# Linear attention feeding a GEGLU block: all of the first batch's q read ahead of the weights, two tiles normalised at once, and a new order of the weight loads

## The chip, the cores and the metric

The kernel runs on 1 core of one Trainium2 chip. The metric is device microseconds (us) of one execution; the profiled span is about 2 us shorter than the time of the same execution. The five engines are called as in the profile: PE (TensorE), DVE (VectorE), ACT (ScalarE), POOL (GpSimd) and SP (SyncE, here only an issuer of transfers).

## The reference

Eight batches of eight heads, 576 positions, 64 channels. A linear ("cosformer") attention is followed by a GEGLU feed-forward block over all 4608 tokens.

```python
def phi(x, c, s):                       # c, s: cosine and sine of the position
    r = np.maximum(x, 0.0)
    return np.concatenate([r * c, r * s], axis=-1)
q_p, k_p = phi(q, cos_w, sin_w), phi(k, cos_w, sin_w)
kv  = np.einsum('bhsf,bhsd->bhfd', k_p, v)
z   = np.sum(k_p, axis=2)
num = np.einsum('bhsf,bhfd->bhsd', q_p, kv)
den = np.einsum('bhsf,bhf->bhs', q_p, z)[..., None] + 1e-06
x   = (num / den).transpose(0, 2, 1, 3).reshape(B * S, H * D)   # 4608 x 512
out = (gelu(x @ w_gate) * (x @ w_val)) @ w_out                  # 512 -> 1536 -> 512
```

## The kernel before

The tokens are worked through in nine blocks of 512. A block needs the normalised attention output x of its tiles (128 tokens each), turned to channel-first (xT). Then come twelve "gate/value" units (`gv_unit`, PE, then GELU on ACT and a product on DVE) and four output parts (`o_part`, PE) with the third weight, `wo`. Block 0 is the start-up stage: attention of batch 0, the weights and the first gate/value units all compete there. Block 0's output parts are interleaved with attention of batch 1; after that each block's work is interleaved with attention of the next batch.

First, loads are issued from two places. SP loads batch 0, and POOL's queue loads the weights (turning float32 into bfloat16 on the way) and q, k and v of batches 1 and 2:

```python
load(nc.sync, "k", 0, 0, 2); load(nc.sync, "k", 0, 2, 4)
load(nc.sync, "v", 0, 0, 2)
load(nc.sync, "q", 0, 0, NP, 0, 2)                 # two of nine runs of q
# ... v, then two more runs of q
nc.gpsimd.tensor_copy(gate, phi["k", 0][:, 3, 0, 0:1])   # weights start after k is prepared
load_w(0, 2); load_w(2, 2)
load(nc.gpsimd, "q", 0, 0, NP, JA, R)              # the other five runs of q
load_w(4, 2); load_w(6, 2); load_w(8, 2); load_w(10, 2)
# ... q(1), k(1), wo rows 0-3, v(1), wo rows 4-7, q(2)
for m in (0, 2):
    cast_v(1, m, m + 2, pool_copy)                 # v(1) to bfloat16, on POOL itself
# ... wo rows 8-11, k(2), v(2)
```

A "run" of q is the part that belongs to one ninth of the 576 positions (`R` is nine, `JA` four), and q(1) stands for q of batch 1. A "row" of `wo` is 128 of its 1536 rows, so an output part of four rows is four matmuls. POOL works in program order. Its issue of a transfer waits until the eighth transfer before it has landed (the releasers in the trace show it), so POOL's waits tell when transfers landed.

Second, the preparation of q and k: per batch, nine cosine operations on DVE and nine sine operations on ACT, each 128x256, float32 in and bfloat16 out.

Third, the order of work between block 0's last gate/value unit and block 1:

```python
order = (
    [("o", 0, 0), ("k",), ("o", 1, 0), ("q", 0), ("o", 2, 0), ("q", 1), ("o", 3, 0)]
    + [("o", 0, 4), ("q", 2), ("o", 1, 4), ("kv",), ("q2", 0, 5), ("o", 2, 4)]   # o(t, 4): wo rows 4-7
    + [("nm", 0, 6), ("o", 3, 4), ("nm", 1, 2), ("o", 0, 8), ...]
    # ...
    + [("xt", 2, 4), ("xt", 3, 0), ("o", 3, 8), ("q2", 5, 9)])
# ... "k": k(1) preparations; "q": q(1) turned on PE, copied by DVE or ACT; "q2": sines of q(2) on ACT
# ... "kv": the k-v product; "nm": attention of one tile (PE), normalised on DVE; "xt": x turned on PE
prep("q", 2, 0, range(R))          # nine cosines of q(2) on DVE
cast_v(2, 0, 2, pool_copy)
cast_v(2, 2, 4, pool_copy)
```

Fourth, what block 1 starts with. SP turns q of batch 2 by two transposing transfers and then loads batch 3:

```python
if n == 1 and jt == 0:
    turn_x(1, NT - 1)
    turn_q(b)          # two dma_start_transpose on SP, from qp(2) to qT(2)
    loads(b + 1)       # q(3), k(3), v(3), on SP behind them
```

## Time and profile before

| | before |
|---|---|
| time, median of 3 runs | 333.44 us (333.24 to 333.95) |
| profiled span | 331.5 us |
| PE busy | 320.4 us (97%) |
| chain of waits that ended last | 84% PE, 6% DMA, 5% DVE |
| first gate/value matmul of block 0 | 14.60 us |
| first output matmul of block 0 | 44.30 us |

The page of before, cut to its head and its chain of waits. The columns of the engine lines are busy time, share of the span and number of instructions.

```profile
span 331.5 us, 6342 instructions
...
PE 320.4 (97%) x2441; PEld 163.2 (49%) x2441; DVE 172.3 (52%) x416; ACT 159.7 (48%) x340; POOL 27.2 (8%) x44
...
PE 84%; DMA 6%; DVE 5%; ACT 2%; POOL 1%; issue 1%; SPq 0%; DVEq 0%
```

PE bounds the kernel, so the time can fall only where PE idles or does dummy matmuls (on a tile of zeros; nobody reads the result). That is the first 44 us, and a few waits after them. The timeline of before: its columns are start (us), length (us), engine, line, operation, count, and in brackets the idle time before and what ended it.

```profile
14.60 0.60 PE L349 MATMUL ps<-xT,wg_sb 128*128 128x128 bf16 x4
...
30.93 0.75 POOL L98 DMA_DIRECT2D wo_sb<-in_moe_w_out_dram  x1 [0.62 <-DMA wv_sb<-in_moe_w_val_dram]
...
42.10 1.15 POOL L179 CAST vx<-vf 128x1152 bf16<-128x1152 f32 x1 [7.13 <-DMA vf<-in_v_dram]
42.31 1.33 DVE L162 TENSOR_SCALAR qp<-qf,cos_t 128x256 bf16<-128x256 f32 x2
43.58 1.15 POOL L179 CAST vx<-vf 128x1152 bf16<-128x1152 f32 x1 [0.34 <-DMA vf<-in_v_dram]
44.30 1.89 PE L375 MATMUL ps<-wo_sb,hT 128*128 128x512 bf16 x8
...
46.15 2.97 DVE L162 TENSOR_SCALAR kp<-kf,cos_t 128x256 bf16<-128x256 f32 x9
47.78 1.89 PE L375 MATMUL ps<-wo_sb,hT 128*128 128x512 bf16 x8
50.30 0.38 PE L204 MATMUL ps<-ident,qp 128*128 128x128 bf16 x4 [0.63 <-DVE qT L433]
51.48 1.33 PE L241 MATMUL ps<-vx,kp 64*128 64x65 bf16 x72
...
60.05 2.45 DVE L162 TENSOR_SCALAR qp<-qf,cos_t 128x256 bf16<-128x256 f32 x9
62.73 8.37 SPq L193 DMA_TRANSPOSE qT<-qp  x2
75.15 0.40 PE L282 MATMUL ps<-kv_sb,qT 128*128 128x65 bf16 x7 [1.09 <-DMA qT<-qp]
```

DVE prepares the cosines of q(2) in 2.45 us, and when the last is done SP issues the transposes of q(2) at 62.73 us. PE needs their result at 74.1 us and gets it at 75.15 us.

### The profile page before, as it was taken

Reading aid. Unit: us, or ns where it says so; the run is one execution under the profiler, and the core shown is the slowest. Engines: PE = TensorE matmul, PEld = TensorE weight load, DVE = VectorE, ACT = ScalarE, POOL = GpSimd, SP = SyncE. Lnnn points to the kernel's source line nnn. Section 1 sums busy time; section 2 is a strip of 40 time slices with the busy share of each in tenths; the row PEclk is TensorE's granted clock in tenths of the full one; section 3 lists DMA queues with packets and bytes.
Section 4 is the critical chain, followed back from the end, with each engine's and each line's share of the span. In section 5 each row is a group of like instructions: output and inputs, shape, how many; then the busy total and the mean of one; then the engine's idle time right before and its main releaser. Section 6 shows DMA issues by size and latency. Waiting matters only on the chain.

```text
span 331.5 us, 6342 instructions
## 1 busy us (share of the span) xinstructions
PE 320.4 (97%) x2441; PEld 163.2 (49%) x2441; DVE 172.3 (52%) x416; ACT 159.7 (48%) x340; POOL 27.2 (8%) x44
## 2 busy tenths in 40 slices
PE   8888999999999999999999999999999999999995
PEld 3577555445455445544554455445544444444443
DVE  5776595848846854755375537562632322223211
ACT  8654584957653752754365436553232222322220
POOL 2954161100000000000000000000000000000000
PEclk9999999999999999999999999999999999999999
DMA  7999998799599999979947995780421221111124
GB/s 268 194 235 289 277 301 309 139 147 367 113 146 368 168 134 335 254 119 239 330 80 118 228 334 81 122 128 13 81 55 38 45 47 32 34 32 32 34 64 95
DMA packets 67918, 53.24 MB, mean 161 GB/s; under 512 B 44080, under 2 KB 53040, under 8 KB 67888
## 3 DMA queue, kind: packets, MB, share of 16 engines
q1 hardware_dynamic: 57936, 40.25, 52.0%
q0 software_dynamic: 9792, 12.45, 16.5%
q8 instruction: 19, 0.31, 0.4%
q10 hardware_dynamic: 160, 0.13, 0.2%
q14 instruction: 11, 0.09, 0.1%
HBM read 37.75 MB, written 9.44 MB: 142 GB/s over the span
## 4 chain that ended last, share of the span: by engine, by line
PE 84%; DMA 6%; DVE 5%; ACT 2%; POOL 1%; issue 1%; SPq 0%; DVEq 0%
PE ps L349 51%; PE ps L375 26%; PE ps L282 3%; DMA qT<-qp 3%; PE ps L241 2%; DMA wv_sb<-in_moe_w_val_dram 2%; DMA kf<-in_k_dram 1%; DVE kp L169 1%; DVE kp L162 1%; DVE qp L162 1%; PE ps L626 1%; DVE hT L358 1%; ACT kp L160 1%; POOL wg_sb L94 1%; DVE qT L433 0%
## 5 line engine op out<-in xcount | busy, mean ns | idle before, releaser
L358 DVE TENSOR_TENSOR hT<-gel,ps 128x512 bf16<-128x512 f32 (+2 forms) x119 | 75.9, 638 | 133.5 <-PE ps L349 129.7
L357 ACT ACTIVATE gel<-ps 128x512 f32<-128x512 f32 (+2 forms) x119 | 66.4, 558 | 114.8 <-PE ps L349 114.3
L349 PE MATMUL ps<-xT,wv_sb 128*128 128x512 bf16 (+2 forms) x476 | 112.8, 359 | 1.2 <-DMA wv_sb<-in_moe_w_val_dram 0.9
L349 PE MATMUL ps<-xT,wg_sb 128*128 128x512 bf16 (+2 forms) x476 | 112.9, 359 | 1.0 <-DVE xT L334 0.7
L375 PE MATMUL ps<-wo_sb,hT 128*128 128x512 bf16 x420 | 106.0, 379 | 0.1
L349 PEld LDWEIGHTS <-wv_sb 128*128 128x128 bf16 x476 | 45.5, 98 | 49.7 <-DMA wv_sb<-in_moe_w_val_dram 1.1
L349 PEld LDWEIGHTS <-wg_sb 128*128 128x128 bf16 x476 | 44.8, 98 | 48.1 <-issue 0.9
L375 PEld LDWEIGHTS <-hT 128*128 128x128 bf16 x420 | 38.4, 98 | 41.0 <-issue 0.4
L384 ACT COPY o_sb<-ps 128x512 f32<-128x512 f32 x34 | 20.0, 587 | 31.8 <-PE ps L375 31.8
L160 ACT ACTIVATE qp<-qf,sin_t 128x256 bf16<-128x256 f32 x70 | 30.7, 502 | 0.4 <-DMA qf<-in_q_dram 0.4
L160 ACT ACTIVATE kp<-kf,sin_t 128x256 bf16<-128x256 f32 (+1 forms) x75 | 30.5, 482 | 0.7 <-DMA kf<-in_k_dram 0.7
L295 DVE TENSOR_TENSOR x_sb<-ps,rec 128x512 bf16<-128x512 f32 x39 | 27.0, 691 | 1.3
L162 DVE TENSOR_SCALAR qp<-qf,cos_t 128x256 bf16<-128x256 f32 x72 | 22.6, 366 | 0.1
L282 PEld LDWEIGHTS <-qT 128*128 128x128 bf16 x312 | 15.0, 98 | 9.1 <-DMA qT<-qp 1.4
L162 DVE TENSOR_SCALAR kp<-kf,cos_t 128x256 bf16<-128x256 f32 x63 | 18.7, 355 | 0.0
L282 PE MATMUL ps<-kv_sb,qT 128*128 128x65 bf16 x312 | 16.8, 194 | 1.2 <-DMA qT<-qp 1.1
L140 PE MATMUL ps<-dummy 128*128 128x512 bf16 x33 | 10.1, 439 | 1.5 <-POOL dummy L114 1.5
L250 ACT CAST kv_sb<-ps 128x260 bf16<-128x260 f32 x14 | 4.6, 382 | 13.0 <-PE ps L241 13.0
L241 PEld LDWEIGHTS <-kp 64*128 64x128 bf16 x504 | 8.5, 94 | 3.0 <-issue 3.0
L179 DVE CAST vx<-vf 128x1152 bf16<-128x1152 f32 (+2 forms) x13 | 9.6, 737 | 0.6 <-DMA vf<-in_v_dram 0.5
L241 PE MATMUL ps<-vx,kp 64*128 64x65 bf16 x504 | 9.3, 191 | 0.0
L294 DVE RECIPROCAL rec<-den 128x8 f32<-128x8 f32 x39 | 7.9, 203 | 1.3
(57 smaller groups left out, 92.8 us busy)
## 6 DMA issues: line engine op xcount, KB each, us to landing
out_dram<-o_sb SPq DMA_DIRECT2D x70, 128.0 KB, 2.4
kf<-in_k_dram SPq DMA_DIRECT2D x12, 576.0 KB, 6.6
vf<-in_v_dram SPq DMA_DIRECT2D x11, 576.0 KB, 9.3
qf<-in_q_dram SPq DMA_DIRECT2D x10, 576.0 KB, 5.2
qf<-in_q_dram POOLq DMA_DIRECT2D x4, 576.0 KB, 12.8
kf<-in_k_dram POOLq DMA_DIRECT2D x4, 576.0 KB, 9.8
vf<-in_v_dram POOLq DMA_DIRECT2D x4, 576.0 KB, 12.2
wg_sb<-in_moe_w_gate_dram POOLq DMA_DIRECT2D x6, 256.0 KB, 9.2
```

The lines of the kernel that those rows point to most:

```text
L140: nc.tensor.matmul(bank(to), lhsT=dummy[:, 0:128], rhs=dummy, start=True, stop=True)
L160: nc.scalar.activation(o, i, AF.Relu, scale=tab[:, j:j + 1])
L162: (eng or nc.vector).tensor_scalar(o, i, 0.0, tab[:, j:j + 1], op0=ALU.max, op1=ALU.mult)
L179: copy(vx_tiles[b % 2][:, m0:m1, j0:j1, 0:D], staged["v", b][:, m0:m1, j0 * D:j1 * D].rearrange("p m (j d) -> p m j d", d=D),)
L241: nc.tensor.matmul(bank(6 + i)[:, m * (D + 1):(m + 1) * (D + 1)], lhsT=kp[rr, m, j, :], rhs=vx[rr, m, j, :], start=(j == 0), stop=(j == R ...
L282: nc.tensor.matmul(bank(b0 + h // 4)[:, (h % 4) * (D + 1):(h % 4 + 1) * (D + 1)], lhsT=q_cols(b, t, h), rhs=kv_sb[b][:, h // 2, h % 2, :], ...
L295: nc.vector.tensor_tensor(x, nm[:, :, :, 0:D], rec[:, :, :, None].to_broadcast([128, 2, 4, D]), op=ALU.mult,)
L349: nc.tensor.matmul(bank(b0 + g)[:, 0:w], lhsT=wt[:, ct, js], rhs=xt[:, ct, c0:c0 + w], start=(ct == 0), stop=(ct == CT - 1),)
L357: nc.scalar.activation(gel[:, 0:w], bank(b0)[:, 0:w], AF.Gelu)
L358: nc.vector.tensor_mul(hT[n][:, jt, c0:c0 + w], gel[:, 0:w], bank(b0 + 1)[:, 0:w])
L375: nc.tensor.matmul(bank(to), lhsT=hT[n][:, jt, tt * 128:(tt + 1) * 128], rhs=wo_sb[:, jt, :], start=(jt == 0), stop=(jt == JT - 1),)
L384: copy(o_sb, bank(to))
```

## The change

Its intent: in block 0, read all of q before any weight, so that attention of tiles 0 to 3 can be done while the weights land; normalise tiles 0 and 1 together; gate the weights on the first cast of v instead of on k; and load `wo` ahead of batch 2. The diff, cut to its core:

```diff
     load(nc.sync, "k", 0, 0, 2)
     load(nc.sync, "k", 0, 2, 4)
+    load(nc.sync, "q", 0, 0, NP, 0, JA)
     load(nc.sync, "v", 0, 0, 2)
-    load(nc.sync, "q", 0, 0, NP, 0, 2)
-    ... (v in two pieces, q runs 2-3)
+    load(nc.sync, "v", 0, 2, 4)
+    load(nc.sync, "q", 0, 0, NP, JA, R)
...
+    def nm_pair(b, t, firsts):      # matmuls of two tiles into four banks
+        ...
+        nc.vector.tensor_scalar_add(den, nm[:, :, :, D], EPS)     # 128 x 16
+        nc.vector.reciprocal(rec, den)
+        ...                         # one product per tile
...
-    nc.gpsimd.tensor_copy(gate, phi["k", 0][:, 3, 0, 0:1])
+    nc.gpsimd.tensor_copy(gate, vx_tiles[0][:, 0, 0, 0:1])
     load_w(0, 2)
     load_w(2, 2)
-    load(nc.gpsimd, "q", 0, 0, NP, JA, R)
-    load_w(4, 2) ... load_w(10, 2)
-    # then q(1), k(1), wo 0-3, v(1), wo 4-7, q(2), [cast v(1)], wo 8-11, k(2), v(2)
+    for part in range(2):
+        prep("q", 0, part, (8,), eng=nc.gpsimd)
+    for jt in (4, 6, 8, 10):
+        load_w(jt, 2)
+    # then q(1), wo 0-3, k(1), v(1), wo 4-7, wo 8-11, q(2), k(2), v(2), [cast v(1)]
...
     # block 0: the new order of PE's work
+    nm_pair(0, 0, (6, 4))
+    ... (all eight q transposes, x transposes of tiles 0 and 1, nm of tile 2)
     gv_unit(0, 0, 0, 128)
     gv_unit(0, 1, 0, 128)
+    nm_unit(0, 3, 6)
+    gv_unit(0, 0, 128, 128)
+    gv_unit(0, 1, 128, 128)
+    gv_unit(0, 2, 0, HALF) ...      # units of 256 and 512 columns from here on
```

From block 0's first output part on, the order of PE's work is the same in both kernels.

## The prediction

> **What bounds the kernel now.** TensorE. The page gives PE 97% busy (320.4 of 331.5 us) at full granted clock; the chain of waits is 84% PE. From 44.2 us, where block 0's last gate/value matmul ends on PE's timeline, the order is the same in both kernels. Up to there the useful PE work is about 20.7 us of gate/value matmuls (12 x 1.73) plus about 6.5 us of attention and transposes. The rest is start-up: nothing useful before 9.36 us, first gate/value matmul at 14.60 us, and some 4 us of holes after that (0.93 us on a value weight at 18.2, 0.7 us on an xT copy at 27.9, about 1.5 us where 128-column units wait for PSUM banks).
>
> **What the change does.** It moves all work of tiles 0-1 (q transposes of runs 0-7, normalisation, x transposes) before the first gate/value unit. nm_pair saves one 0.17 us add and one 0.20 us reciprocal. Preparing run 8 of q moves to POOL. 33 dummies become 30 (0.22 us each when warm).
>
> Costs: the weights are gated on the first cast of v instead of k. In the trace 576 KB land on the SP queue per 1.9 us (k half 4.6, v half 8.4 us). In the new order I estimate: q part 1 at 8.2, v halves at 10.1 and 12.0, q part 2 at 14.2 to 15.2 us (it then shares the DMA engines with the weights; the Trainium skill, "DMA: Bandwidth & Descriptors", section "Queues, rings and completion order", says each DMA engine round-robins between queue rows; no run here shows the split). The weights start at about 11.0 instead of 8.2 us, but total bytes are equal, so the last weight pair lands near 30.5 us as before (30.9, from POOL's waits).
>
> The new critical path is DVE: after q part 2 it does five preparations (0.31 each), the pair's add and reciprocal (0.45), two multiplies (0.69, 0.62), a qT copy (0.4); then PE's nm of tile 2 (0.26) and a dummy. That puts the first gate/value unit at 18.5 to 19.4 us, 4 to 5 us LATER than now. After it remain 20.7 + about 2.3 us of PE work and about 0.8 us of holes (PSUM banks, while DVE does nm of tiles 2 and 3): 23.8 us. Block 0 then ends at 42.3 to 43.2 instead of 44.2 us: gain 1 to 2 us.
>
> **Afterwards.** wo rows 4-11 land before q of batch 2, which I estimate at 51.8 instead of 49.5 us, just when ACT wants it (53.4 less the shift). The waits on qT (0.6 us at 50.3 on DVE, 1.1 us at 75.1 on the DMA transpose) shift and stay. Net there 0 to -0.5 us.
>
> **Predicted: 331.9 us, 8 in 10 between 330.5 and 333.4.** Faster by over 2% 0.02, within 2% 0.965, slower 0.015.
>
> **Right or wrong by:** first gate/value matmul at 18.5-19.4 us on PE's timeline, hardly any hole over 0.5 us after 22 us; the pair normalisation starting at 15.8-16.8 us behind the q preparations; no PE wait on weights; block 0 ending at 42-43 us; the 75 us wait moved by the same shift.
>
> **What would make it wrong:** q part 2 much later than 15 us or weights late (gain lost); q part 2 at 13.5 us (gain over 2.5 us); PE's clock falling in the sparse stretch 9 to 18 us (the Trainium skill, "TensorE: Matmul & The Clock Gate", Part 1, names idle windows of about 3.4 us; the before trace shows no drop with holes under 0.9 us); q of batch 2 late enough to widen the 75 us wait.

## More of the kernel before

At 44.30 us PE starts block 0's output parts. The second half of the group at 47.78 us, from about 48.65 us, is the first use of `wo` rows 4-7. Those were issued by POOL at 30.93 us, and PE does not wait for them.

(The two casts on POOL, at 42.10 and 43.58 us, will matter later. Beside the first, two cosines of q(1) took 1.33 us, where the pair before them took 0.61; the cosines of k(1) come behind both casts.)

## The result, and the profile after

| | before | after |
|---|---|---|
| time, median | 333.38 us (4 runs, 333.24 to 333.95) | 333.65 us (4 runs, 333.51 to 334.12) |
| ratio, with its 95% interval | | 1.0007 (0.999 to 1.0025) |
| profiled span | 331.5 us | 331.6 us |
| first gate/value matmul of block 0 | 14.60 us | 17.71 us |
| first output matmul of block 0 | 44.30 us | 40.80 us |
| SP issues the transposes of q(2) | 62.73 us | 63.13 us |

A ratio here is the mean time of one kernel's fast runs over the mean of the other's in the same rounds, so it is not quite the ratio of the medians quoted. The time did not move: the predicted gain of 1.5 us is absent, although the start gained 3.5 us. The page of after:

```profile
span 331.6 us, 6186 instructions
...
PE 317.8 (96%) x2360; PEld 161.0 (49%) x2398; DVE 169.1 (51%) x400; ACT 159.8 (48%) x335; POOL 29.0 (9%) x45
...
PE 78%; DMA 13%; POOL 3%; ACT 2%; issue 1%; DVE 1%; SPq 0%; DVEq 0%
```

More of the chain of waits now runs through transfers (13%, after 6%), 5% of the span through a load of `wo`. Such a share counts a transfer from its issue on and is not PE's wait; PE's waits are read off the timeline. (Part of the fall in PE's busy time is matmul records missing from the trace; the waits below don't rest on it.) The timeline of after:

```profile
15.17 0.16 DVE L316 TENSOR_SCALAR den<-ps 128x16 f32<-128x16 f32 x1
...
17.71 0.39 PE L375 MATMUL ps<-xT,wg_sb 128*128 128x128 bf16 x4
...
32.07 0.75 POOL L98 DMA_DIRECT2D wo_sb<-in_moe_w_out_dram  x1 [0.64 <-DMA wv_sb<-in_moe_w_val_dram]
...
40.80 1.89 PE L401 MATMUL ps<-wo_sb,hT 128*128 128x512 bf16 x8
...
42.63 2.62 DVE L161 TENSOR_SCALAR kp<-kf,cos_t 128x256 bf16<-128x256 f32 x9
...
46.20 2.25 POOL L178 CAST vx<-vf 128x1152 bf16<-128x1152 f32 x2
47.62 1.86 PE L401 MATMUL ps<-wo_sb,hT 128*128 128x512 bf16 x4 [2.31 <-DMA wo_sb<-in_moe_w_out_dram]
49.71 1.59 PE L401 MATMUL ps<-wo_sb,hT 128*128 128x512 bf16 x4
51.24 1.33 PE L240 MATMUL ps<-vx,kp 64*128 64x65 bf16 x72
...
58.27 1.15 POOL L178 CAST vx<-vf 128x1152 bf16<-128x1152 f32 x1 [9.81 <-PE ps L401]
59.58 1.15 POOL L178 CAST vx<-vf 128x1152 bf16<-128x1152 f32 x1 [0.16 <-DMA vf<-in_v_dram]
59.81 3.16 DVE L161 TENSOR_SCALAR qp<-qf,cos_t 128x256 bf16<-128x256 f32 x9
63.13 8.26 SPq L192 DMA_TRANSPOSE qT<-qp  x2
75.25 0.40 PE L281 MATMUL ps<-kv_sb,qT 128*128 128x65 bf16 x7 [1.42 <-DMA qT<-qp]
```

The lead of after over before, read off the same work in the two traces, goes like this:

- First output part: 44.30 less 40.80, 3.50 us ahead.
- First use of `wo` rows 4-7: before at about 48.65 us, after at 47.62 us, 1.03 us ahead. PE stood for 2.31 us, because those rows landed at 47.6 us. They were issued 1.14 us later than before (32.07 against 30.93 us), and PE now wanted them at 45.3 us.
- The k-v product: 51.48 less 51.24, 0.24 us ahead. The output part behind the hole took 1.86 us and the next 1.59 us, where four such matmuls take 1.03 us. Before, in its turn, had a 0.63 us wait here that after does not have.
- The issue of q(2)'s transposes: 62.73 less 63.13, 0.40 us behind. DVE's nine cosines began 0.24 us earlier, but they took 3.16 instead of 2.45 us, while POOL cast v(2).
- First use of the transposed q(2): 75.15 against 75.25 us. PE now waits 1.42 instead of 1.09 us. Nothing of the lead is left.

The slow matmuls have their reason in the clock. This is the view by windows of after; the columns are window, length, busy time and instructions of PE, PE's weight loads, DVE, ACT and POOL, then granted clock, DMA share and GB/s.

```profile
46.00:47.00 1.00, 0.00 (x0) 0.00 (x0) 0.38 (x1) 0.00 (x0) 1.00 (x2) 1.00 1.25 213
47.00:48.00 1.00, 0.38 (x1) 0.10 (x1) 0.00 (x0) 0.00 (x0) 1.00 (x2) 0.72 1.21 260
48.00:49.00 1.00, 1.00 (x4) 0.43 (x3) 0.00 (x0) 0.00 (x0) 0.45 (x1) 0.50 1.16 379
49.00:50.00 1.00, 1.00 (x7) 0.58 (x6) 0.05 (x1) 0.00 (x0) 0.00 (x0) 0.50 1.00 393
50.00:51.00 1.00, 1.00 (x4) 0.29 (x2) 0.38 (x1) 0.00 (x0) 0.00 (x0) 0.57 1.05 415
```

After the hole the granted clock is half for about 3.4 us. The lost clock in these windows adds up to 0.28 + 0.50 + 0.50 + 0.43 = 1.71 us, or 0.5% of the span, and indeed three of the four runs of after have a mean granted clock of 0.994 or 0.995.

### The profile page after: what moved, and what is told of

Its sections match the earlier page's. It is cut to its first block, busy times and chain, and to the rows that moved or that the text cites. A ratio compares the mean times of both kernels' runs of the same rounds, so it can differ in the third digit from the quotient of the medians.

```text
span 331.6 us, 6186 instructions
## 1 busy us (share of the span) xinstructions
PE 317.8 (96%) x2360; PEld 161.0 (49%) x2398; DVE 169.1 (51%) x400; ACT 159.8 (48%) x335; POOL 29.0 (9%) x45
## 3 DMA queue, kind: packets, MB, share of 16 engines
q0 software_dynamic: 9648, 11.80, 15.8%
## 4 chain that ended last, share of the span: by engine, by line
PE 78%; DMA 13%; POOL 3%; ACT 2%; issue 1%; DVE 1%; SPq 0%; DVEq 0%
PE ps L375 46%; PE ps L401 26%; DMA wo_sb<-in_moe_w_out_dram 5%; DMA wv_sb<-in_moe_w_val_dram 3%; PE ps L281 3%; DMA qT<-qp 3%; PE ps L240 2%; DMA vf<-in_v_dram 2%; POOL wg_sb L94 1%; POOL wv_sb L95 1%; PE ps L624 1%; POOL qp L161 1%; ACT qp L159 1%; ACT gel L383 1%; ACT kp L159 0%
## 5 line engine op out<-in xcount | busy, mean ns | idle before, releaser
L384 DVE TENSOR_TENSOR hT<-gel,ps 128x512 bf16<-128x512 f32 (+2 forms) x114 | 75.0, 660 | 133.0 <-PE ps L375 131.7
L383 ACT ACTIVATE gel<-ps 128x512 f32<-128x512 f32 (+2 forms) x114 | 65.6, 575 | 112.0 <-PE ps L375 109.9
L375 PE MATMUL ps<-xT,wg_sb 128*128 128x512 bf16 (+2 forms) x451 | 111.5, 368 | 0.5
L375 PE MATMUL ps<-xT,wv_sb 128*128 128x512 bf16 (+2 forms) x445 | 110.5, 368 | 0.4
L401 PE MATMUL ps<-wo_sb,hT 128*128 128x512 bf16 x400 | 104.5, 383 | 3.7 <-DMA wo_sb<-in_moe_w_out_dram 2.3
L375 PEld LDWEIGHTS <-wv_sb 128*128 128x128 bf16 x456 | 44.0, 98 | 49.6 <-DMA wv_sb<-in_moe_w_val_dram 0.3
L375 PEld LDWEIGHTS <-wg_sb 128*128 128x128 bf16 x456 | 43.4, 98 | 47.4 <-issue 0.3
L410 ACT COPY o_sb<-ps 128x512 f32<-128x512 f32 x34 | 20.0, 588 | 31.6 <-PE ps L401 30.5
L159 ACT ACTIVATE kp<-kf,sin_t 128x256 bf16<-128x256 f32 (+1 forms) x75 | 30.5, 483 | 0.3 <-DMA kf<-in_k_dram 0.3
L139 PE MATMUL ps<-dummy 128*128 128x512 bf16 x28 | 9.1, 484 | 1.5 <-POOL dummy L113 1.5
L178 DVE CAST vx<-vf 128x1152 bf16<-128x1152 f32 x12 | 9.2, 770 | 0.8 <-DMA vf<-in_v_dram 0.8
L292 DVE TENSOR_SCALAR den<-ps 128x8 f32<-128x8 f32 x38 | 6.1, 160 | 5.1 <-PE ps L281 5.0
## 6 DMA issues: line engine op xcount, KB each, us to landing
vf<-in_v_dram POOLq DMA_DIRECT2D x4, 576.0 KB, 14.2
```

The costliest lines, as they stand in the source:

```text
L139: nc.tensor.matmul(bank(to), lhsT=dummy[:, 0:128], rhs=dummy, start=True, stop=True)
L159: nc.scalar.activation(o, i, AF.Relu, scale=tab[:, j:j + 1])
L178: copy(vx_tiles[b % 2][:, m0:m1, j0:j1, 0:D], staged["v", b][:, m0:m1, j0 * D:j1 * D].rearrange("p m (j d) -> p m j d", d=D),)
L375: nc.tensor.matmul(bank(b0 + g)[:, 0:w], lhsT=wt[:, ct, js], rhs=xt[:, ct, c0:c0 + w], start=(ct == 0), stop=(ct == CT - 1),)
L383: nc.scalar.activation(gel[:, 0:w], bank(b0)[:, 0:w], AF.Gelu)
L384: nc.vector.tensor_mul(hT[n][:, jt, c0:c0 + w], gel[:, 0:w], bank(b0 + 1)[:, 0:w])
```

## The experiments

**Theories.** Q: PE's lead is given back because other streams do not start earlier, namely the loads on POOL's queue and the work that hangs on them, and the end of the span is set by those. In its simplest form the one hole on `wo` rows 4-7 is the whole loss. R: the loss lies elsewhere (the half clock; the single late chain that ends in q(2)'s transposes; the new order of loads as such; POOL's extra work), and removing the `wo` wait changes nothing. In what follows T is the time at which SP issues the transposes of q(2), and "before" is the kernel before on the same chip in the same rounds. All edits are to the kernel after, unless said otherwise.

### 1. The wait for wo rows 4-7: load them earlier (wo4_early)

```diff
-    for name in ("k", "v"):
-        for m in (0, 2):
-            load(nc.gpsimd, name, 1, m, m + 2)
+    for m in (0, 2):
+        load(nc.gpsimd, "k", 1, m, m + 2)
     load_wo(4, 4)
+    for m in (0, 2):
+        load(nc.gpsimd, "v", 1, m, m + 2)
```

> The changed kernel with one edit: wo rows 4-7 are loaded ahead of v of batch 1 instead of behind it. Theory Q (the load queue: the 3.4 us won by 41 us is handed back because wo rows 4-7 land at 47.5 us, behind q, wo 0-3, k and v of batch 1): the rows land at about 43.8 us, PE's 2.3 us wait for them and the half clock at 48-51 us are gone; instead v of batch 1 lands near 47.4 us and PE waits 0.5 to 1.5 us for its cast before the kv of batch 1. Time 330.5 to 332.3. Rival R (what sets the time is the DMA transpose of q of batch 2, landing at 75.2 us whatever came before, with PE waiting for it): the wait at 75 us grows by what was won, time 333.3 to 333.8.

Measured 332.67 us (332.11 to 333.73), ratio 0.9961 (0.9929 to 0.9993). The `wo` wait is gone, but against before only 0.9 us (medians) to 1.3 us (the ratio) came of it, a little less than expected. PE now waits 0.5 us for POOL's cast of v(1), 0.6 us for an output copy that stands behind ACT's sines of q(2), and 1.3 us for an x tile at 80.15 us. T moved from 63.13 us (62.21 in the control of experiment 4) only to 61.59 us. The wait is a part of the loss; it isn't the whole.

### 2. The half clock: fill the hole with dummies (warm_hole)

```diff
         if what == "o":
             o_part(...)
+        if (what, *a) == ("o", 3, 0):
+            dummies(10, 2)
```

> The changed kernel with 10 dummy matmuls (2.2 us) put into PE's hole before wo rows 4-7, so that the clock does not fall. Theory C (the half clock at 48-51 us is a loss of its own, about 1.5 us of PE time): clock 1.00 throughout, time 332.0 to 332.6. Theory R (absorbed: one of the four runs of the changed kernel had the clock at 1.00 and was no faster, 333.7): clock 1.00, PE reaches the nm of batch 2 about 1.4 us earlier and waits that much longer there, time 333.2 to 333.8.

Measured 333.62 us (332.94 to 334.89), ratio 0.9985 (0.9948 to 1.0022). The granted clock stayed at 1.00 through the stretch, and the output part behind it took its normal time. Yet the end did not come earlier: T was 62.24 us, and PE waited 0.5 us for a qT copy and 1.6 us for an x tile later. So the half clock costs nothing of its own that five rounds can see (the interval reaches 0.5% below before); what it takes, a later wait would take. This trace also shows a second thing: one sine preparation of k(1) on DVE, normally 0.34 us, lasted 2.91 us from 45.42 us, while POOL cast v(1) from 45.93 to 48.18 us. I come back to it in experiment 8.

### 3. POOL's preparation of run 8 (run8_back) and the order of loads (old_order)

```diff
# run8_back
-    for part in range(2):
-        prep("q", 0, part, (8,), eng=nc.gpsimd)
...
     gv_unit(0, 3, 0, HALF)
+    prep("q", 0, 0, (8,))
+    prep("q", 0, 1, (8,), eng=nc.scalar)

# old_order: the kernel after with before's order of POOL's loads behind the weights
-    # q(1), wo 0-3, k(1), v(1), wo 4-7, wo 8-11, q(2), k(2), v(2), [cast v(1)]
+    # q(1), k(1), wo 0-3, v(1), wo 4-7, q(2), [cast v(1)], wo 8-11, k(2), v(2)
```

> The changed kernel with run 8 of q prepared on VectorE and ScalarE behind the first half block, as before, not on POOL ahead of the third weight pair. Theory Q: the weight issue is not held for 2.6 us at 14.0-16.6 us, the DMA stream runs about 0.7 us earlier, wo rows 4-7 land near 46.8 us, PE's wait for them shrinks from 2.3 to about 1.6 us; time 332.7 to 333.4. If POOL's detour cost the stream nothing (the four weights in flight kept it busy), the wait stays at 2.3 us and the time at 333.6.

Measured 332.90 us (332.63 to 334.36), ratio 0.9973 (0.994 to 1.0006). With POOL free, the weights and all behind them came about 1.1 us earlier, and the `wo` wait fell from 2.31 to 1.45 us. But POOL's casts came earlier too (45.10 us) and met the nine cosines of k(1), which took 5.05 us instead of 2.62; PE then waited 1.1 us for a qT copy, and the half clock came anyway.

> The changed kernel with POOL's load order of before from batch 1 on (q, k, wo 0-3, v, wo 4-7, q of batch 2, the casts of v, wo 8-11, k, v). wo 4-7 stands behind the same bytes in both orders, so Theory Q says: it lands at 47.5 us again, the same 2.3 us wait and half clock; the reordering did not make the hole. q of batch 2 lands about 2.5 us earlier and the transposes of q of batch 2 may start up to 0.4 us sooner: time 333.1 to 333.7. If the reordering itself is to blame, the wait goes away and the time is under 332.

Measured 333.52 us (332.72 to 334.18), ratio 0.9982 (0.995 to 1.0014). Going back to the old order does not bring the missing gain. My expectation of an unchanged 2.3 us wait was wrong: it was 1.28 us. Rows 4-7 landed 1.2 us earlier here, behind the same transfers as in after. Most of that may be scatter: four other runs with after's loads waited 1.51 to 1.87 us (after_again, v2_cast_dve, q2cos_late, cast1_act), so the 2.31 us of the first profile is the extreme. One difference stays untested: after's POOL had issued k(2) and half of v(2) by 43.41 us, while rows 4-7 were still on their way; in old_order they come behind the casts, from 45.82 us.

### 4. A control, and T moved alone (after_again, q2cos_late, v2_cast_dve)

after_again is the kernel after, unchanged, on the chip of the other two.

> The changed kernel itself, unedited, as the control on the same chip as the next three. Every theory: 333.4 to 334.1, a wait of 1.5 to 2.5 us for wo rows 4-7 at about 45 us, the DMA transposes of q of batch 2 issued at about 63 us.

Measured 334.24 us (332.94 to 334.72), ratio 0.9993 (0.9963 to 1.0022). The profiled execution had a different mixture of waits than the first one: 1.64 us for `wo`, 0.85 us for a qT copy, no half clock, 1.90 us for an x tile at 81.35 us, and only 0.2 us for the transposed q(2). The sum comes to much the same. A single hole is not a stable property of this kernel, so none of them is likely to be the whole cause. The x tile stands behind ACT, which waited 1.86 us for q(3), until 77.75 us. SP had issued that load at 71.28 us, behind the transposes of q(2), so this wait hangs on T as well.

```diff
# q2cos_late: the last of nine cosines of q(2), and all that hangs on it, one step later
-    prep("q", 2, 0, range(R))
+    prep("q", 2, 0, range(R - 1))
...
                 if n <= 2 and jt < 3:
                     prep_third("k", b, jt)
+                if n == 1 and jt == 0:
+                    prep("q", 2, 0, (R - 1,))
+                    turn_q(b)
+                    loads(b + 1)

# v2_cast_dve: v(2) cast on DVE in units 2 and 3 of block 1
-    cast_v(2, 0, 2, pool_copy)
-    cast_v(2, 2, 4, pool_copy)
...
+                if n == 1 and jt in (2, 3):
+                    cast_v(b, 2 * jt - 4, 2 * jt - 2, dve_copy)
```

> The changed kernel with the last (ninth) cosine preparation of q of batch 2 moved on VectorE behind the first k third of batch 2, some 1.8 us later; nothing else depends on it but the DMA transposes of q of batch 2. Theory T (in all six profiles so far the end of the kernel follows the issue of those transposes, within about 0.7 us: before 62.7 us, after 63.1, wo rows earlier 61.6): issue at 64.7 to 65.1 us, PE's wait for the transposed q grows from 1.4 to about 3 us, time 1.4 to 2.0 us above the control. Rival (PE's own work and holes up to 60 us set the time, the transposes only follow): wait grows but is regained, time within 0.5 us of the control.

Measured 335.83 us (334.88 to 336.97), ratio 1.0045 (1.0014 to 1.0076), 1.6 us above the control. T was 63.35 us, 1.1 us later than in the control, where I had expected 1.8. The first use of the transposed q(2) in the control, then T and that use in q2cos_late:

```profile
72.91 0.40 PE L281 MATMUL ps<-kv_sb,qT 128*128 128x65 bf16 x7 [0.21 <-DMA qT<-qp]
...
63.35 9.49 SPq L192 DMA_TRANSPOSE qT<-qp  x2
73.99 0.40 PE L281 MATMUL ps<-kv_sb,qT 128*128 128x65 bf16 x7 [1.70 <-DMA qT<-qp]
```

PE's own work is untouched by this edit, and each of its six runs is slower than each of the control's. So what SP issues at T does hold the end: the transposes, and the loads of batch 3 that stand behind them. The two are not separated.

> The changed kernel with the cast of v of batch 2 taken off POOL and put on VectorE in gate/value units 2 and 3 of block 1, where VectorE has room. Theory L (a POOL cast holds VectorE's preparations up: nine cosine preparations took 3.16 us beside it, 2.45 us without): they take 2.4 to 2.5 us, the transposes of q of batch 2 are issued at about 62.4 to 62.7 us instead of 63.1, time 0.3 to 0.7 us below the control. If the lock is not it: 3.1 us again, no change.

Measured 332.75 us (331.97 to 334.81), ratio 0.9966 (0.993 to 1.0002), in the medians 1.5 us below the control; I had expected 0.3 to 0.7. In the means it is 0.9 us, since two of the six runs, at 334.67 and 334.81 us, gained nothing. The nine cosines of q(2) took 2.44 us as before the change, and T was 61.40 us. POOL's cast of v(2) beside them is probably a second part of the loss; the interval just reaches 1.

### 5. The hole removed without touching a load (wo_no_wait)

This kernel is wrong (relative error 0.28): block 0 multiplies with rows 0-3 of `wo` where it should use rows 4-7. All loads are as in after.

```diff
-                rhs=wo_sb[:, jt, :],
+                rhs=wo_sb[:, jt % 4 if n == 0 and 4 <= jt < 8 else jt, :],
```

> The changed kernel, wrong on purpose: block 0 multiplies with wo rows 0-3 again where it should use rows 4-7, so it does not wait for them; every load stays where it was. Isolates the wait. Theory Q with T: the 1.6 to 2.3 us wait goes, but VectorE's k preparations (held by the POOL cast of v) then hold the copy of qT and PE waits 1.5 us or more there; the transposes of q of batch 2 are issued at 61.0 to 62.3 us instead of 62.2 to 63.1; time 0 to 1.0 us below the control (332.9 to 333.8 where before is 333.5). If the wait for wo alone ate the 3.4 us: 330.5 to 331.5.

Measured 333.96 us (333.14 to 334.87), ratio 1.0014 (0.9997 to 1.003): no gain at all. The timeline of this kernel shows where the hole went.

```profile
53.44 2.10 ACT L159 ACTIVATE qp<-qf,sin_t 128x256 bf16<-128x256 f32 x5 [3.33 <-DMA qf<-in_q_dram]
55.45 1.04 ACT L410 COPY o_sb<-ps 128x512 f32<-128x512 f32 x2
56.06 0.38 PE L356 MATMUL ps<-ident,x_sb 128*128 128x128 bf16 x4 [2.29 <-ACT o_sb L410]
...
63.23 8.28 SPq L192 DMA_TRANSPOSE qT<-qp  x2
```

ACT works in program order. It reached the sines of q(2) early, stood 3.33 us until q(2) landed at 53.4 us, did five sines, and only then copied the output parts out of the banks that PE needed. PE's hole of 2.31 us reappears as one of 2.29 us, again with a reduced clock behind it, and T is where it was. PE is faster up to a fixed arrival, whichever load arrives next. I had expected the cast of v(1) to be what holds PE here. It was not: the cast began at 46.38 us, when the preparations of k(1) were done.

### 6. The new load order alone, and the old gate (before_new_order, gate_k)

```diff
# before_new_order: the kernel before with after's order of POOL's loads and casts
# gate_k: the kernel after
-    nc.gpsimd.tensor_copy(gate, vx_tiles[0][:, 0, 0, 0:1])
+    nc.gpsimd.tensor_copy(gate, phi["k", 0][:, 3, 0, 0:1])
```

> The kernel BEFORE with only the new load order on POOL's queue (wo rows 8-11 ahead of batch 2, casts of v last). Theory: the order by itself wins nothing, since PE there comes to wo rows 4-7 at 48.6 us, after they land; v and q of batch 2 land later and the POOL casts of v of batch 2 move on to VectorE's cosines of q. Time 0 to 0.8 us above before, no wait for wo rows.

Measured 334.43 us (333.88 to 337.4), ratio 1.0037 (1.0009 to 1.0066). By itself the new order costs about 0.9 us in the medians, slightly more than expected: v(1) is now cast at 44.62 us, where one cosine of q(1), begun at 44.89 us, is held for 2.13 us, and PE waits 1.15 us for it.

> The changed kernel with the weight loads gated on the preparation of k, as before, so that they start at about 8 instead of 10.7 us. Theory Q: the DMA engines' gap at 11-13 us closes, the stream runs 0.5 to 1.2 us earlier and the wait for wo rows 4-7 shrinks to about 1 us, but q part 2 and v share the engines and land 0.5 to 1.5 us later, so block 0 ends that much later. Time within 0.7 us of the control. If the late gate was the cause of the lost gain: 331.5 or less.

Measured 332.90 us (331.37 to 334.0), ratio 0.9978 (0.9957 to 0.9999). The weights' issue moves from 10.71 to 8.09 us, the first gate/value matmul from 17.71 to 16.87 us and the first output part from 40.80 to 39.87 us, yet the median gains only some 0.6 us against before. The `wo` wait is down to 0.72 us and a DVE wait of 1.66 us stands in its place: again k(1)'s cosines beside POOL's casts, 5.07 us. (The trace is of the fastest of the six runs, 331.37 us; the next was at 332.56.)

### 7. All holders taken away (best1, best2, best3, best2_again)

best1 combines wo4_early, run8_back and v2_cast_dve with two more edits; best2 also moves ACT's sines of q(2) out of the way of the output copies; best3 is best2 with gate_k's edit.

```diff
# best1, besides wo4_early, run8_back and v2_cast_dve
-    for m in (0, 2):
-        cast_v(1, m, m + 2, pool_copy)
...     # behind the second group of q(1) transposes in the order
+            if a[0] == 1:
+                for m in (0, 2):
+                    cast_v(1, m, m + 2, act_copy)
...     # preparation of q(3) one unit later in block 1
-        t_kv, t_nm, t_q, t_k = {1: (4, 6, 7, 12), ...
+        t_kv, t_nm, t_q, t_k = {1: (4, 6, 8, 12), ...

# best2, besides best1: the sines of q(2) behind the first copies, two of them on DVE
-    ("kv",), ("q2", 0, 5), ("o", 2, 4) ... ("o", 1, 8) ... ("o", 3, 8), ("q2", 5, 9)
+    ("kv",), ("o", 2, 4) ... ("o", 1, 8), ("q2", 0, 3) ... ("o", 3, 8), ("q2", 3, 7)
     prep("q", 2, 0, range(R))
+    prep("q", 2, 1, (7, 8))
```

> A version meant to beat both: the changed kernel with wo rows 4-7 ahead of v of batch 1, run 8 of q off POOL, the cast of v of batch 1 on ScalarE and that of batch 2 on VectorE, and the preparation of q of batch 3 one unit later. Theories Q, L and T together: no wait for wo rows, none over 0.4 us for the casts, transposes of q of batch 2 issued at 60.0 to 61.0 us; time 330.3 to 331.5. If the end is set elsewhere: 332.5 or more.

Measured 331.09 us (330.59 to 331.61), ratio 0.9906 (0.9877 to 0.9936), T at 60.27 us. The wait of experiment 5 is left: PE stands 1.8 us for output copies behind ACT's sines.

> best1 with ScalarE's sines of q of batch 2 moved behind the first two output copies (best1 held PE 1.8 us there) and two of the nine sines on VectorE. Theory T: PE's 1.8 us wait is gone but only an earlier issue of the transposes counts: 59.3 to 60.3 us against 60.27, time 330.2 to 331.2. If PE's wait itself counted: 329.3 to 329.9.

Measured 329.30 us (328.71 to 330.04, 4 runs), ratio 0.9866 (0.9847 to 0.9885), outputs correct. The timeline of best2:

```profile
41.18 1.89 PE L401 MATMUL ps<-wo_sb,hT 128*128 128x512 bf16 x8
...
42.85 2.45 DVE L161 TENSOR_SCALAR kp<-kf,cos_t 128x256 bf16<-128x256 f32 x9
...
47.65 1.33 PE L240 MATMUL ps<-vx,kp 64*128 64x65 bf16 x72
...
56.23 2.44 DVE L161 TENSOR_SCALAR qp<-qf,cos_t 128x256 bf16<-128x256 f32 x9
59.72 8.29 SPq L192 DMA_TRANSPOSE qT<-qp  x2
72.02 0.40 PE L281 MATMUL ps<-kv_sb,qT 128*128 128x65 bf16 x7 [0.64 <-DMA qT<-qp]
```

Here the lead of the start is kept. Against before it is 3.12 us at the first output part (44.30 less 41.18), 3.0 us at T (62.73 less 59.72), 3.13 us at the transposed q(2), and 3.3 us at the end of the span (331.5 less 328.2).

One expectation failed here. If only T counted, the time was to be 330.2 to 331.2 us; if PE's wait of 1.8 us in best1 counted by itself, 329.3 to 329.9. T came where I had put it, yet the time came at the edge of the second range: against best1 the ratio fell by 0.0040, or 1.3 us, while T and the span of the profiled executions fell by 0.5 us. (best2's was the slowest of its four runs.) So T, read off one execution, does not tell the median to better than a microsecond.

> best2 a second time, on the same chip as best3, since its first job gave only four runs: 328.7 to 330.1 where before is near 333.5, ratio 0.985 to 0.990.

Measured 329.49 us (328.89 to 330.67), ratio 0.9874 (0.9845 to 0.9903), on another chip: best2 holds.

> best2 with the weight loads gated on k as in the kernel before (start at about 8 us, the DMA gap at 11-13 us closed). Theory Q: the stream runs about 1 us earlier, q of batch 2 lands earlier, first gate/value unit at about 16.9 us, transposes issued at 58.7 to 59.5 us, time 0.3 to 1.2 us below best2 on the same chip.

Measured 329.43 us (328.81 to 330.56), ratio 0.9863 (0.9833 to 0.9893): no clear gain over best2 in the same rounds (0.06 us in the medians, 0.4 in the ratios), where I had hoped for 0.3 to 1.2 us. Its first output part, at 41.55 us, was not earlier than that of best2 (41.18 us), so the start gain seen in gate_k does not show there. But its profiled execution is not a typical one: it was the slowest of the six, the granted clock was 0.50 from 11.2 to 14.6 us, and the first gate/value matmul came at 18.55 us (17.31 in best2). The four runs with a mean clock of 1.00 lay between 328.81 and 329.85 us, so a gain of some tenths is not excluded.

### 8. Which holders are enough (wo_last, wo_last_cast, cast1_act, both)

best2 changes six things at once. The last four kernels ask for the smallest set. wo_last is wrong (relative error 0.37): block 0 uses rows 0-3 of `wo` three times, and rows 4-11 are loaded last, so that neither the `wo` wait nor the late q(2) can hold PE. cast1_act is the kernel after with v(1) cast on ACT as in best1; wo_last_cast and both add this edit to wo_last and to wo4_early.

```diff
# wo_last
-                rhs=wo_sb[:, jt, :],
+                rhs=wo_sb[:, jt % 4 if n == 0 else jt, :],
...
-    load_wo(4, 4)
-    load_wo(8, 4)
     for name in ("q", "k", "v"):
         for m in (0, 2):
             load(nc.gpsimd, name, 2, m, m + 2)
+    load_wo(4, 4)
+    load_wo(8, 4)
```

> The changed kernel, wrong on purpose: block 0 multiplies with wo rows 0-3 three times, and rows 4-11 (2 MB read) are loaded last on POOL's queue, behind batch 2, where nothing waits for them in time. It takes from the stream what stands between v of batch 1 and q of batch 2. If the load stream as a whole is what ate the 3.4 us: no wait for wo rows, none for q of batch 2 (which lands about 47 to 49 instead of 52 to 53.4 us, so ScalarE is not held as in wo_no_wait), the DMA transposes of q of batch 2 issued at 60.0 to 61.3 us, time 330.8 to 332.0. If the time stays at 333.3 or more, the stream is not the cause.

Measured 334.19 us (330.68 to 335.0), ratio 0.9997 (0.9956 to 1.0039). My expectation failed clearly. PE has no wait on a load left between 40 and 90 us, and still nothing is gained. The view of the tile of prepared k in wo_last, with durations in ns as minimum, median and maximum, and then its timeline:

```profile
L161 DVE TENSOR_SCALAR kp<-kf,cos_t x9: 334/341/2806, 42.9 to 45.2; 128x256 bf16<-128x256 f32 x9
```

```profile
45.62 2.25 POOL L178 CAST vx<-vf 128x1152 bf16<-128x1152 f32 x2
49.20 0.38 PE L203 MATMUL ps<-ident,qp 128*128 128x128 bf16 x4 [2.66 <-DVE qT L455]
63.14 8.11 SPq L192 DMA_TRANSPOSE qT<-qp  x2
```

The median of the nine cosines is 0.34 us. The last, begun at 45.22 us, takes 2.81 us, to 48.02 us, which is 0.15 us after the end of POOL's second cast (47.87 us). PE then waits 2.66 us for the qT copy that DVE owes it, and the clock halves again. In warm_hole, run8_back, gate_k and before_new_order the held operation also ends 0.15 to 0.16 us after the end of the second cast, so the pair of casts holds it.

> wo_last (wrong on purpose, 2 MB of wo rows out of the way) with the cast of v of batch 1 on ScalarE instead of POOL. In wo_last no load held PE any more, yet five of six runs stayed at 333.7 to 335.0 and one was at 330.68: VectorE's nine k preparations took 5.13 us there beside POOL's 2.25 us of casts, and PE waited 2.66 us for the copy of qT behind them. Theory QL (two holders side by side, the load stream and POOL's casts; only with both gone does the gain show): k preparations 2.4 to 2.6 us, no wait over 0.6 us for qT, all runs between 330.0 and 331.5. If it stays at 333 or more, neither is the cause.

Measured 330.11 us (329.31 to 330.86), ratio 0.9872 (0.9846 to 0.9898). This edit moves POOL's casts of v(1) to ACT, and nothing else differs from wo_last. The timeline of wo_last_cast:

```profile
43.48 2.83 DVE L161 TENSOR_SCALAR kp<-kf,cos_t 128x256 bf16<-128x256 f32 x9
...
47.48 0.38 PE L203 MATMUL ps<-ident,qp 128*128 128x128 bf16 x4 [0.30 <-DVE qT L453]
...
59.93 8.30 SPq L192 DMA_TRANSPOSE qT<-qp  x2
```

With the cosines back at 2.83 us, PE waits 0.3 us for the copy, and T falls by 3.2 us. So with PE's load waits gone, moving the cast of v(1) is worth some 4 us (the two ratios differ by 0.0125, which is 4.2 us of 333.5). That is about what wo_last's trace shows behind the cast: 2.4 us more of waiting, and 3.4 us at half clock, which cost PE up to 1.7.

> The changed kernel with only the cast of v of batch 1 on ScalarE. Theory QL: VectorE is not held, but PE still waits 1.6 to 2.3 us for wo rows 4-7 and q of batch 2 still lands at 52 to 53.5 us; time 0 to 0.8 us below the changed kernel, 332.7 to 333.7 where before is 333.5. If the casts alone were the cause: 331.5 or less.

Measured 333.27 us (331.58 to 333.9), ratio 0.9965 (0.9934 to 0.9997): with the load waits in place, the same edit is worth about 1 us. The `wo` wait is 1.5 us, and later PE waits for the transposed q(2) for 1.7 us.

> The changed kernel with wo rows 4-7 ahead of v of batch 1 and the cast of v of batch 1 on ScalarE, nothing else; with wo4_early and cast1_act it completes the square. Theory QL: 330.9 to 332.2, lower than either edit alone.

Measured 332.54 us (331.8 to 333.23), ratio 0.9946 (0.992 to 0.9971), just above the range that I expected. The early `wo` rows and the moved cast leave ACT waiting 2.8 us for q(2), PE 1.8 us for an output copy, and q(2)'s cosines at 3.47 us beside POOL's cast of v(2). So these two holders are not enough for a kernel with right results: the q(2) arrival and the cast of v(2) hold it next.

### What the runs say together

Times are medians; T and the span less T come from the one profiled execution of each kernel.

| run | what it removes | time (median) | before beside it | T, us | span less T, us |
|---|---|---|---|---|---|
| before | | 333.38 | | 62.73 | 268.8 |
| after | | 333.65 | 333.38 | 63.13 | 268.5 |
| wo_no_wait | `wo` wait | 333.96 | 333.50 | 63.23 | 269.2 |
| wo_last | all load waits of PE | 334.19 | 333.53 | 63.14 | 268.7 |
| cast1_act | cast of v(1) on POOL | 333.27 | 334.26 | 61.21 | 269.0 |
| both | `wo` wait, cast of v(1) | 332.54 | 334.26 | 62.10 | 268.6 |
| q2cos_late | nothing; delays T | 335.83 | 334.25 | 63.35 | 269.9 |
| v2_cast_dve | cast of v(2) on POOL | 332.75 | 334.25 | 61.40 | 268.7 |
| wo_last_cast | all load waits of PE, cast of v(1) | 330.11 | 334.26 | 59.93 | 268.8 |
| best2 | `wo` wait, q(2) ahead of copies, all POOL casts | 329.30 | 333.50 | 59.72 | 268.5 |

In the 20 profiled executions the span less T lies between 268.2 and 269.9 us (mean 268.7, standard deviation 0.4), while the first output part ranges from 39.9 to 44.3 us. So what follows T takes nearly the same time in all, and a change to the start counts by about what it moves T. That this is cause and not just company rests mainly on q2cos_late, which delays T and what SP issues behind it, and little else; even there the span less T is 0.9 us longer than in its control. v2_cast_dve points the same way with less certainty.

## Why the prediction was wrong

**Right: the mechanism of the start.** I predicted that the first gate/value matmul would come later and block 0 would end earlier all the same, with hardly any hole over 0.5 us after 22 us. It came 3.1 us later, block 0 ended 3.5 us earlier, and PE had 23.84 us of work in the 24 us from 20 to 44 us. The class, within 2%, was right too, but by little merit: the forecast gain at the start and the loss that I had not foreseen cancel.

**Mis-sized: the start.** "Block 0 then ends at 42.3 to 43.2" was too late by 1.5 to 2.4 us: 40.80 us. The first gate/value matmul, predicted for 18.5 to 19.4 us, came at 17.71 us. From there block 0 took 23.09 us, where the prediction had 23.8; that is 0.7 us of it. The larger term that was off is "q part 2 at 14.2 to 15.2 us": DVE began on it at 13.00 us. I had drawn on the Trainium skill, "DMA: Bandwidth & Descriptors", section "Queues, rings and completion order" (DMA engines alternate between queue rows packet by packet), and counted on q sharing the engines with weights. The trace does not show much of that: the windows from 11 to 13 us move only 155 and 63 GB/s, after 363 GB/s in the one before. The weight stream, issued from 10.71 us, had not got under way when q was done. Every step behind q moved up with it: the pair normalisation, for example, began at 15.17 us instead of 15.8 to 16.8 us. I had listed this case ("gain over 2.5 us").

**The step that failed: what lies behind block 0.** The prediction said "no PE wait on weights", that the waits at 50 and 75 us "shift and stay", and "Net there 0 to -0.5 us". That treats everything after 44 us as one PE chain that slides with PE. It isn't one. The forecast start gain was more than met (3.5 us against 1 to 2), and the net behind it was a loss of 3.6 us (the span is 0.1 us longer in the end). Three things did not slide:

- *The loads on POOL's queue.* `wo` rows 4-7 landed at 47.6 us, while PE wanted them at 45.3 us. Before, PE came to them only at about 48.65 us and did not wait. Their issue was 1.14 us later than before (32.07 against 30.93 us), and it waited for the last weight, which the prediction had landing "near 30.5 us as before": the weights opened 2.4 us later (10.71 against 8.30 us), and POOL's two preparations of run 8 occupied it for 2.6 us in the middle of the weight issues (without these two, run8_back waits 1.45 us for the rows; with the old gate, gate_k waits 0.72). Behind them, q(2), estimated at 51.8 us, arrived only at 53.4 us where ACT stood waiting for it (wo_no_wait). That run shows that a PE without the first wait meets the second.
- *POOL's casts of v.* Where they meet a DVE preparation, they hold it until about 0.15 us after their end. In the first profile of after the cast of v(1) met none (46.20 us, the cosines of k(1) were done by 45.25) and that of v(2) cost 0.7 us of DVE; in after_again the cast of v(1) led to a wait of 0.85 us. wo_last against wo_last_cast shows some 4 us for v(1), once the load waits are away; v2_cast_dve shows 0.9 to 1.5 us for v(2) in the kernel after, at the edge of the noise. I had not looked at this collision at all. In before it was cheap by its timing alone: v(1) was cast at 42.1 and 43.6 us, beside two cosines of q(1) (1.33 us instead of 0.61) and before those of k(1) at 46.15 us; PE's only wait near it is the 0.63 us at 50.30 us. v(2) was cast at 55.9 and 58.3 us, before the q(2) cosines at 60.05 us. A PE that is ahead pulls DVE's preparations forward, and POOL's casts, which stand behind the loads of batch 2 in the new order, came later: 46.20 us.
- *The transposes of q(2), as the sum of both.* They were the one 75 us wait whose widening I had named as a risk, and "the 75 us wait moved by the same shift" was wrong: it stayed at 75.25 us against 75.15 us.

**What the lead bought in place of a gain.** Removing a single holder gives between nothing (wo_no_wait, wo_last) and 1.5 us (v2_cast_dve, medians); removing the load waits together with the cast of v(1) gives 4.2 us (wo_last_cast, 334.26 less 330.11), and the whole set gives 4.2 us with right results (best2, 333.50 less 329.30). The holders run side by side and let go of PE at nearly the same time, so that where one is removed the next takes over.

**The half clock** looked like the obvious culprit and wasn't. warm_hole kept the clock at 1.00 and gained nothing measurable. The risk that I had named, the clock falling between 9 and 18 us, did not occur in the profile of after either (granted clock 1.00 there). It is a real one, though: in the profiled executions of best3 and wo_last_cast the clock was 0.50 from about 11.2 to 14.7 us.

**What stays open.** How the 3.5 us divide among the holders cannot be given as a sum, since they overlap. Why `wo` rows 4-7 landed earlier in old_order than in after is not settled, nor is the share of the transposes and of the loads behind them in what T holds, nor why the first output part scatters by a microsecond among kernels with the same start. wo_last had one run of 330.68 us with a granted clock of 1.00, among five of 333.65 us and more; that the cast and the cosines just missed each other in it is my reading, but only the first run has a trace. And I did not try best2's rearrangements on the kernel before, so how much of its 4.2 us needs the new start is not shown by a run. Two numbers bound it. The lead that best2 keeps is 3.1 us at the first output part. And from 44 to 100 us PE idles for only 1.8 us in the trace of before, and from 100 to 326 us not at all, so an estimate of what the same edits could win there is at most 1.8 us.

## What to carry to other kernels

When a change pulls the bounding engine ahead, list every stream that does not move with it (loads already queued at their limit, casts, transposes issued elsewhere), write down for each when it arrives and when it will now be wanted, and credit only the gain that is left behind the last of them. If removing one wait changes nothing, the next one is probably standing right behind it: remove them together before concluding that none mattered. A marker like T, an event after which all runs take nearly equal time, tells quickly which gains can count.

## What the Trainium skill lacked or had wrong

- "SBUF — State Buffer", section "Who interferes with whom", says that `tensor_scalar` and casts on DVE can take a port pair shared with GpSimd, and that the loser blocks for the whole instruction. The traces agree with the blocking (0.34 us became 2.81 us in wo_last). What it lacks: the block here outlasted one instruction. The held operation came free only 0.15 us after the second of two back-to-back casts (2.25 us together), so two casts in a row cost their sum here; in old_order, where the casts began 1.94 us apart, no DVE preparation took over 1.31 us. It also began 0.4 us before the first cast's record, which the page does not explain, and no run here does (spans on POOL are rough in these profiles).
- "TensorE: Matmul & The Clock Gate", Part 1, gives the half-rate state "after ≥1 idle window (~3.4µs)". Here idle stretches of 2.29, 2.31 and 2.66 us were enough for a reduced clock of some 3.4 us (granted clock 0.50 from 48 to 50 us in after); two of 1.45 and 1.11 us close together also did it (run8_back), while 1.64 and 0.85 us in after_again did not. In the 3.41 us before each drop PE was busy for 0.75 (wo_last), 1.09 (wo_no_wait), 1.15 (run8_back), 1.28 (after), 1.48 (best3) and 1.85 us (wo_last_cast), so the clock fell though PE worked in up to half of the stretch; where the limit lies, no run here shows. The page says that the window runs free of the program; how little activity in it counts as idle is not said.
- "DMA: Bandwidth & Descriptors", section "Issuing engines are not separate DMA queues", calls the sequencer time of starting a DMA "usually small relative to the DMA itself". For the two DMA transposes of q(2), SP's queue was taken for 8.0 to 9.5 us in all runs, of about 12 us from first issue to PE's use, and the loads behind them waited for that.
- "GPSIMD Engine Reference", section "4.1 Engine selection", calls one-input elementwise work on GpSimd roughly line-rate. The two preparations of 128x256 elements on POOL took 1.49 and 1.13 us in after, against 0.34 us on DVE. DVE worked beside them, so part of that can be waiting, and spans on POOL are rough.
